# Score products on the diagonal 64x64 quarters of TensorE, V products on the other two, and 274 tiles kept off ScalarE

## The chip, the cores and the metric

The kernel runs on one core of a Trainium2 chip. The metric is the device time of one execution in microseconds (us); the time given is the median of three runs. One more execution was taken with the hardware profiler, and the trace is of that one.

## The reference, cut to what matters

The input is one image of 224 x 224 positions with C = 96 channels. Each position gives a query, a key and a value of 96 channels; the first 48 channels attend inside horizontal strips of 8 x 224 positions, the other 48 inside vertical ones.

```
sw, C2 = 8, C // 2
qkv = einsum('bhwc,cd->bhwd', x, wqkv);  q, k, v = three slices of C channels
# horizontal: 28 strips of 1792 positions, 48 channels
ah = softmax(einsum('bqc,bkc->bqk', qh, kh) * C2**-0.5)
oh = einsum('bqk,bkc->bqc', ah, vh)
# vertical: the same on 28 strips of 224 x 8 positions, the other 48 channels
ov = ...
out = einsum('bhwc,cd->bhwd', concat(oh, ov), wo)
```

In all, 56 strips of 1792 x 1792 scores, each of which needs an exponential: 180 million of them. The row sums come out of the V product, whose 49th column is a one.

## The kernel before, in words

**Tiling.** Two strips make a *pair* P; there are 28 pairs, 0 to 13 horizontal and 14 to 27 vertical. The keys and queries of the two strips of a pair lie on partitions 0 to 48 and 64 to 112 of `KT_sb` and `QT_sb` (index w = 0, 1). The queries of a pair are cut into four chunks c of 512, 512, 512 and 256. A *tile* is 128 keys x 512 queries x 2 strips (256 keys in the last chunk): 128 x 1024 scores in two PSUM banks. There are 49 tiles in a pair and 1372 in all.

**A tile on ScalarE.** TensorE makes the scores with four matmuls, one on each 64 x 64 quarter of its array (`qk_fn`, L761: strip w on 64 rows, key half kh on 64 columns). ScalarE takes exp of both banks at once into a bf16 tile `PT` (L939). TensorE then multiplies with V (`pv_fn`, L788): 128 keys on all 128 rows, one strip on 64 columns and the other on the other 64, so two matmuls a tile, which add up in one bank over the tiles of a chunk. ScalarE's tiles use two sets of two banks in turn (`SETS`), so that the scores of tile n+2 wait until ScalarE is through with tile n. The other four banks are a ring (`RING`): the bank in which the V product adds up, the score banks of the tiles off ScalarE, and the banks of the *fills*.

**A tile off ScalarE.** 251 tiles get their exponential elsewhere, as integer arithmetic on the bits of the scores. The table `KINDS` names them, a letter each. All of them make their scores twice (`s_fn`, L774). Kind P (155 tiles): VectorE pass 1 takes the low halves of the words into `qb` (L1082), GpSimd squares (L1110), adds a constant (L1111) and squares again (L1106); the scores are made again and VectorE pass 2 adds them in (L1087). Kind R (96 tiles) has a pass more on VectorE (L1084) and only one square on GpSimd.

**Fills** are the other products: keys, queries and values of the pair after the one at work (L589, L634), and the output projection (L703, from pair 14 on). VectorE copies each out of its bank.

**What sets the order.** `ORDER` has a string per pair; a letter is one step of TensorE: `q` scores of a ScalarE tile, `1` and `2` (or `3`, `4`) first and second scores of a tile off ScalarE, `v` one V product, `k`, `g`, `f` a fill. TensorE runs them exactly so. The orders of VectorE and GpSimd come from a planner in the program, which walks `ORDER` with durations and picks what is ready. Each engine waits on counters of the others, `emit` writes those waits, and every wait holds up all that is behind it on the engine.

Of the kernel before, what the change touches and what calls it, by code (L numbers as in the profile page):

```python
# [6 lines left out]
BF16 = mybir.dt.bfloat16  # L7
# [21 lines left out]
    ["PR", "P", "PPP", ""],  # L29
    ["RPR", "PP", "RRPRR", ""],  # L30
    ["PR", "P", "PPRR", ""],
    ["RRPP", "RP", "PRRP", ""],
    ["RP", "RP", "PPPRR", ""],
    ["PRR", "P", "PPPRR", ""],
    ["PPRR", "P", "PRPRP", ""],
    ["PRR", "P", "PPRP", ""],
    ["PR", "RRP", "PPPRRP", ""],
    ["RR", "PP", "PPRRP", ""],
    ["PRP", "PPPR", "RP", ""],
    ["RP", "P", "RPPPRR", ""],  # L40
    ["RPR", "P", "PPPRPR", ""],
    ["RRP", "P", "PPRRP", ""],
    ["PR", "RPPPR", "PR", ""],
    ["PP", "RRPPR", "P", ""],
    ["PPPR", "RPP", "RRPP", ""],
    ["PR", "PPPRP", "P", ""],
    ["PPR", "R", "PPRP", ""],
    ["PPPRR", "PP", "R", ""],
    ["PPPP", "RR", "PRPP", ""],
    ["PPR", "R", "PPPP", ""],  # L50
    ["PPP", "RRRPR", "PP", ""],
    ["PPR", "PP", "RRPP", ""],
    ["PR", "PPP", "RRPP", ""],
    ["PP", "PP", "PRR", ""],
    ["PPP", "RRPR", "RPP", ""],
    ["PP", "P", "PPRRPPP", ""],
]
NPT = 28
NQB = 5
NV2 = 1  # L60
# [7 lines left out]
SEMD, SEMP, SELF, SEMX = 0.15, 0.10, 0.19, 0.05  # L68
# [3 lines left out]
D_H, D_F, D_SQ, D_AF, D_M2 = 0.604, 1.137, 1.9, 1.03, 0.055  # L72
D_AW, D_AG = 2.1, 1.03
# [6 lines left out]
D_V2 = 0.6  # L80
# [15 lines left out]
    "vq2vqv1qvvkqvvvq1vqvkqkvq1qkvqvvq2qvvkqv2qkqkkqkqk1qvvkqvvqv1qvvqvvqv1qvvqkvvq2qvkvqv2qvvq1vvq2qvv2qvq2vvq1qvv2qvvqv2q",
    "vvq1vqvkq2vqkvq1qkvqvvkvq1qvvvqvvq2vqvkvqkqk1qvvq1qvkqkkq1qkvqvvq1vqvvqvv2qvqvvq2vqvv2qvvq2qvv1qvq2vvq1qvv2qvqkvvq1vvq2q",
    "vv2qvqv1qkvqvvvq1vqvkqkvq1qkvvqkvq2vqvkqkvvq1qvvgqkqkvgqgkqkvqv2qvvq2vqv1qvvq2vqv1qvvvqvq1vqvvqvv1qvqv2qkq2qvvq3vqvvq2vvq",
    "2qvv2qvvqkkqkq1vqkvvqvvkq1qvgvqkgqkqkvq2vqv1qvkqkvq1vqgvvqvgq2vqkvqkgvq2vqv2qvvq1vqgvq2vqv1qvvqvvq1vqvvqvv1qvvqgvqgvq1vqvvq2vq",
    "v2qvvq2vqv1qvgvqvvq1vqvvqvv2qvqkvqkvkqkvvq1qvvkq3qkvvq2vqv2qvvq4vqgvq2vqvkq1vqv1qvvqgvqvvqkgqkkqgqgvq1vvq4qkvvq2qkvvq",  # L100
    "2qv1qvvvqv1qvvq2vqvkqk2qvvqgvkq1qkvvqkvq1vqvkqkvqgvq4vqgvq1vqvkqk2qvvqkvq1vqkvqkvgq2vqv2qvvq2vqvgq1vqv1qvvgqvvqv1qvvqvvgqv4qvvq",
    "v1qvvqv2qvvq1vq4qvvkqkq1kqvvkqvvkq2qvvqkvvq3vqvgq4vqgvq2vqv2qvvqkvq1vqv1qgvqvkq2vqv2qkvqkvq1vqkvq1vqvvvqv1qvvqvvkqv4qvvqv4qvvq",
    "v1qvvq2vqv1qvvqk1qvvqkvvqvkqkvqggvqkgqk2qvvvq2vqv3qvvqg2qvvqv1qvgqvkq2vqv1qgvqvkq4vqvgq1vqkkqkvqv1qvvkqvgqvvq1vqvgvqvvq1vqvvq2vq",
    "vvvq2vqv2qvvqkkqk1qvqkvvqvvq2vqvvq1vkqv1qvkqv2qvvqk4qvvqvgq2vqv1qgvqkvq1vqkgqv4qvkqv1qkvqvvqvvq1vqvkvqvvq4vqvvq2vvqv1qvvq",
    "v2qvvq1vqv2qvkqkkqvvkqggqkvqg1qvkqkgqkqkkqkvvq2vqv1qvvq1vqgvq2vqv2qvvqv1qkvvq2vqv2qgvqv1qgvqv2qgvqv1qvvqvvgqv1qvvqvvqv1qvvvqvvq",
    "vvqv2qvvq1vqvkq2kqvvq1qvvkqvvqkvvq2qvv1qkvq3vqvvq2vqv2qgvqgvgqkvqkq2vqkvq1vqkkqv2qgvqv2qvkqv1qvvqkvgq1qgvvqvvq2vqvvq2vvq",
    "1qvvvqv1qvvq2vqv4qvvqk1qvkqvvvq1qvvvqvvq2vqvvqkkvqv1qvvqkgq1vqkvq2vqvkq2vqv1qgvqvkq2vqv4qvvqk1qvvqvkqvvkqgvq1qkvvq2vqv2qvvq",
    "1vqv2qvvqgvq1vqv4qvvqk1qkvqvvqv1qvvqvvq2vqvgqkvqgvkqgvvqk1qvvq1vqkvq2vqkvq2vqv1qgvqvkq2vqv1qvvqg2qvvqkkqgvgqgvqkkvqv2qvvq2vq",
    "v1qvvq1vqv2qvvvq2qvv1qvvqkkq1qvkvqvvkqv1qvqvvvq4qvvvqkgqgkqvvq2vqkvq1vqv1qgvqkvq2vqv2qvkqvkq4vqkvq1vqv1qvvgqvvqv1qvvqvvqgvqv2qvvq",
    "kvvq1vqv2qvvq2vqv1qvgvqvvq1vqvvqvvq1vqvkqkvkqvvq2vqkvqvkgq1vqkvq2vqv1qgvqkvq2vqv2qvgqvkqvgqg1qvvqkkqgvkq2qvkvqv1qvvq2vqv2q",  # L110
    "vvq1vqvvvq2vqv1qvvq1vqvvqv1qvvqvvvq2vqvgqgvqgvq1vqvvq2vqv2qvvq2vqv1qvvfqv1qvfqv2qvfqvvfqvvfqv2qvvfqgvqgvq2vqv2qvvgqfvq4fqqvvvvvfffvvvfff",
# [9 lines left out]
class Sched:  # L121
# [70 lines left out]
    def commit(self, eng, start, dur, lat, fn, reads, writes, fresh=(), tag=""):  # L192
        d = self.deps(eng, reads, writes)
# [24 lines left out]
def bass_standalone__window_attn_cswin__vision_kernel(  # L218
# [28 lines left out]
    with es:  # L247
# [21 lines left out]
        V_sb = [sb(f"V_sb{i}", [128, 2, NKT, CA], BF16) for i in range(2)]  # L269
        V2_sb = [sb(f"V2_sb{i}", [128, 2, NV2, CA], BF16) for i in range(2)]  # L270
# [136 lines left out]
        for i in range(2):  # L407
            pool_now(["vones"], lambda e, i=i: e.memset(V_sb[i][:, :, :, C2:CA], 1.0), 0.2)
# [147 lines left out]

        def wblk(P, kind):
            return {"k": 2, "v": 4}[kind] + ph_of(P)

        def wqT_fill(ph):  # L560
            def pe_fn(e, bk):
                for w in range(2):
                    ins = e.matmul(bk[64 * w:64 * w + 64, 0:C], lhsT=wq_sb[ph][0][0:C, 0, :], rhs=ident[0:C, 0:C],
                                   start=True, stop=True)
# [9 lines left out]
        HALVES = [(0, 64), (64, C + 1)]  # L574
# [3 lines left out]
        def prep_fills(P):  # L578
# [3 lines left out]
            for kind, L in (("k", K), ("q", Q)):  # L582
                for c in range(NCH):
                    q0, qs = CH_Q0[c], CH_SIZES[c]

                    def pe_fn(e, bk, kind=kind, q0=q0, qs=qs):
                        for w in range(2):
                            lw = w_sb[:, wblk(P, "k"), :] if kind == "k" else wq_sb[ph][b][:, w, :]
                            ins = e.matmul(bk[64 * w:64 * w + 64, 0:qs], lhsT=lw, rhs=xT_sb[b][0:C + 1, w, q0:q0 + qs],  # L589
                                           start=True, stop=True)  # L590
                        return ins
# [21 lines left out]
            def pe_fn(e, bk):  # L613
                for w in range(2):
                    for a, z in ((0, 64), (64, 128)):
                        ins = e.matmul(bk[a:z, w * k_n[P]:(w + 1) * k_n[P]], lhsT=wqT[ph][:, w, a:z], rhs=ksum[b][:, 0:k_n[P]], start=True, stop=True)
                return ins
# [7 lines left out]
            for k0 in range(0, 2 * NKT, VS):  # L625
                n = min(VS, 2 * NKT - k0)
                ws = sorted({k0 // NKT, (k0 + n - 1) // NKT})

                def pe_fn(e, bk, k0=k0, n=n):
                    for j in range(n):  # L630
                        w, kt = divmod(k0 + j, NKT)
                        for h in range(2):
                            t0 = kt * 128 + 64 * h
# [1000 lines left out]
```

## Time and profile before

| what | value |
|---|---|
| median of 3 runs | 1047.3 us (1047.17 to 1047.32) |
| the profiled execution, its own time | 1047.03 us |
| its span, first to last instruction | 1045.2 us |
| TensorE (PE) busy | 1024.8 us, 13456 matmuls |
| VectorE (DVE) busy | 1027.6 us |
| ScalarE (ACT) busy | 1034.9 us, of it 1030.3 us in 1121 exponentials |
| GpSimd (POOL) busy | 1001.9 us |
| granted TensorE clock | 0.999 |

A busy share says how much of the span has an instruction of the engine in it. The instructions of one engine overlap at their ends, so the step from one to the next is shorter than the duration of one; a busy share near 100% thus doesn't say by itself which engine sets the pace. The views used below are the page's parts, the timeline (instructions in order, merged where alike: start, length, engine, line, operation, tiles, count), the waits, one source line's instructions, and the stretches.

### The profile page before, as it was taken

To read this page: it belongs to the slowest core of one execution; us is meant where nothing else is said; L and a number is where in the kernel's file an instruction comes from. 1 tells how busy PE (TensorE), PEld (TensorE's weight loads), DVE (VectorE), ACT (ScalarE), POOL (GpSimd) and SP (SyncE) were. 2 spreads that over 40 slices of the span, in tenths; PEclk is the share of its full clock that TensorE was granted. 3 is DMA by queue.
4 is the path that set the end of the run, shared out by engine and by line. 5 is a ranking of instruction groups with operands and counts; after the bars stand their busy time and mean duration, and the time that the engine had idled before them with its cause. 6 is when DMAs were issued, how large, how long until landed. Compare 5 with 4: busy or idle time off the path is not lost.

```text
span 1045.2 us, 33013 instructions
## 1 busy us (share of the span) xinstructions
PE 1024.8 (98%) x13456; PEld 388.6 (37%) x13456; DVE 1027.6 (98%) x1905; ACT 1034.9 (99%) x1131; POOL 1001.9 (96%) x662
## 2 busy tenths in 40 slices
PE   9999999999999999999999999999999999999997
PEld 4333333333333333333333333334333333343333
DVE  8999999999999999999999999999999999999998
ACT  8999999999999999999999999999999999999997
POOL 7999999999999999999999999999999999999997
PEclk9999999999999999999999999999999999999999
DMA  8997718828863774132146355534525542552343
GB/s 175 166 181 126 131 24 140 119 52 125 147 93 71 130 108 81 28 59 59 15 91 114 60 93 103 101 58 94 95 49 104 105 100 44 104 102 49 71 79 60
DMA packets 414199, 96.84 MB, mean 93 GB/s; under 512 B 404928, under 2 KB 411296, under 8 KB 414048
## 3 DMA queue, kind: packets, MB, share of 16 engines
q1 hardware_dynamic: 413376, 94.11, 51.9%
q8 instruction: 105, 1.72, 0.7%
q10 hardware_dynamic: 544, 0.44, 0.1%
q14 instruction: 46, 0.38, 0.1%
q0 software_dynamic: 128, 0.20, 0.1%
HBM read 28.31 MB, written 28.21 MB: 54 GB/s over the span
## 4 chain that ended last, share of the span: by engine, by line
PE 59%; DVE 24%; ACT 8%; issue 4%; POOL 4%; DMA 1%; POOLq 0%; ACTq 0%; SPq 0%; DVEq 0%
PE ps L788 23%; PE ps L761 20%; PE ps L774 10%; ACT PT L939 8%; DVE qb L1082 7%; DVE PT L1087 7%; DVE PT L1084 3%; PE ps L589 3%; DVE KT_sb L594 2%; PE ps L703 2%; POOL PT L1106 2%; PE ps L634 2%; DVE OT_sb L958 1%; DVE QT_sb L603 1%; POOL PT L1110 1%
## 5 line engine op out<-in xcount | busy, mean ns | idle before, releaser
L939 ACT ACTIVATE PT<-ps 128x1024 bf16<-128x1024 f32 x1121 | 1030.3, 1091 | 0.6 <-PE ps L761 0.2
L1106 POOL TENSOR_TENSOR PT<-PT 128x1024 f16<-128x1024 f16 x251 | 470.4, 1893 | 8.6 <-DVE PT L1084 1.0
L788 PE MATMUL ps<-PT,V_sb 128*49 128x512 bf16 (+1 forms) x3136 | 470.1, 362 | 0.3 <-DVE PT L1087 0.2
L761 PE MATMUL ps<-QT_sb,KT_sb 49*64 49x512 bf16 (+1 forms) x5292 | 456.4, 361 | 2.6 <-ACT PT L939 1.5
L1082 DVE TENSOR_SCALAR qb<-ps 128x512 f16<-128x512 int16 x490 | 329.8, 697 | 3.2 <-PE ps L761 0.3
L1087 DVE SCALAR_TENSOR_TENSOR PT<-ps,PT 128x512 uint16<-128x512 f32 (+1 forms) x479 | 323.0, 709 | 5.2 <-PE ps L774 0.9
L1110 POOL TENSOR_TENSOR PT<-qb 128x1024 f16<-128x1024 f16 x155 | 291.9, 1892 | 9.8 <-DVE qb L1082 6.5
L761 PEld LDWEIGHTS ps<-QT_sb,KT_sb 49*64 49x64 bf16 x5292 | 136.9, 104 | 264.0 <-ACT PT L939 240.3
L774 PE MATMUL ps<-QT_sb,KT_sb 54*64 54x512 bf16 (+1 forms) x2008 | 202.6, 394 | 11.7 <-DVE PT L1087 2.7
L788 PEld LDWEIGHTS ps<-PT,V_sb 128*49 128x49 bf16 x3136 | 133.2, 103 | 202.6 <-issue 169.8
L1111 POOL TENSOR_SCALAR PT<-PT 128x1024 f16<-128x1024 f16 x155 | 161.8, 1044 | 13.0
L1084 DVE SCALAR_TENSOR_TENSOR PT<-ps,qb 128x512 f16<-128x512 int16 (+1 forms) x190 | 128.0, 688 | 0.6
L774 PEld LDWEIGHTS ps<-QT_sb,KT_sb 54*64 54x64 bf16 (+1 forms) x2008 | 56.8, 103 | 101.0 <-DVE PT L1087 34.2
L958 DVE CAST OT_sb<-ps 113x512 bf16<-113x512 f32 x111 | 68.5, 617 | 0.1
L603 DVE CAST QT_sb<-ps 128x512 bf16<-128x512 f32 (+1 forms) x111 | 67.5, 615 | 0.1
L594 DVE TENSOR_SCALAR_CACHE_REDUCE KT_sb<-ps 128x512 bf16<-128x512 f32 x108 | 64.4, 616 | 0.0
L709 DVE CAST og<-ps 128x480 bf16<-128x480 f32 x84 | 50.8, 616 | 0.2
L641 DVE CAST V_sb<-ps 128x480 bf16<-128x480 f32 (+1 forms) x84 | 50.8, 617 | 0.1
L589 PE MATMUL ps<-xT_sb,wq_sb 97*64 97x512 bf16 x224 | 41.5, 368 | 0.0
L589 PE MATMUL ps<-xT_sb,w_sb 97*64 97x512 bf16 x224 | 39.8, 369 | 0.0
L634 PEld LDWEIGHTS ps<-w_sb,xT_sb 96*64 96x64 bf16 x1568 | 33.6, 112 | 16.3 <-issue 7.5
L634 PE MATMUL ps<-w_sb,xT_sb 96*64 96x48 bf16 x1568 | 39.3, 190 | 0.0
(67 smaller groups left out, 236.4 us busy)
## 6 DMA issues: line engine op xcount, KB each, us to landing
xT_sb<-xt_dram SPq DMA_DIRECT2D x28, 336.0 KB, 5.2
out_dram<-og SPq DMA_DIRECT2D x190, 48.0 KB, 2.0
xp_dram<-in_x_dram SPq DMA_DIRECT2D x26, 336.0 KB
oc_all<-xp_dram SPq DMA_DIRECT2D x26, 336.0 KB, 4.6
xt_dram<-xT_sb SPq DMA_DIRECT2D x26, 336.0 KB, 6.4
oh_all<-ohn SPq DMA_DIRECT2D x52, 84.0 KB, 2.7
stg<-oh_all SPq DMA_DIRECT2D x13, 336.0 KB, 4.6
xt_dram<-xT_sb SPq DMA_DIRECT2D x4, 168.0 KB, 5.1
```

Of the source, the lines that this page charges most:

```text
L589: ins = e.matmul(bk[64 * w:64 * w + 64, 0:qs], lhsT=lw, rhs=xT_sb[b][0:C + 1, w, q0:q0 + qs], start=True, stop=True)
L634: ins = e.matmul(bk[64 * h:64 * h + 64, j * C2:(j + 1) * C2], lhsT=xT_sb[b][0:C, w, t0:t0 + 64], rhs=w_sb[0:C, wblk(P, "v"), 0:C2], start= ...
L761: ins = e.matmul(bank(SETS[s] + w)[64 * kh:64 * kh + 64, i * t["qs"]:(i + 1) * t["qs"]], lhsT=KT_sb[b][64 * w:64 * w + CA, kt * 128 + 64 * ...
L774: ins = e.matmul(bank(bp[w])[64 * kh:64 * kh + 64, 0:512], lhsT=KT_sb[b][64 * w:64 * w + nr, kt * 128 + 64 * kh:kt * 128 + 64 * kh + 64], ...
L788: ins = e.matmul(bank(pb)[64 * w:64 * w + CA, 0:t["qs"]], lhsT=V2_sb[b][:, w, kt - NKT + NV2, :] if second else V_sb[b][:, w, kt, :], rhs= ...
L939: S.commit("act", 0.0, D_ACT, None, lambda e, s=s, slot=slot: e.activation(PT[slot][:], ps[:, 512 * SETS[s]:512 * SETS[s] + 1024], ACTF.Ex ...
L1082: fn, reads, writes = lambda e: e.tensor_scalar(q, l, m, a, ALU.mult, ALU.add), bk, qk
L1084: fn, reads, writes = lambda e: e.scalar_tensor_tensor(y.bitcast(FP16), l, -RA * 2.0 ** 16, q, ALU.add, ALU.mult), bk + qk, ptk
L1087: fn, reads, writes = lambda e: e.scalar_tensor_tensor(y.bitcast(U16), f, 128.0, y.bitcast(FP16), ALU.mult, ALU.add), bk + ptk, ptk
L1106: square = ("pool", D_SQ, lambda e: e.tensor_tensor(y, y, y, ALU.mult), yk + ["pser"], yk)
L1110: return [("pool", D_SQ, lambda e: e.tensor_tensor(y, q, q, ALU.mult), qk, yk), ("pool", D_AF, lambda e: e.tensor_scalar(y, y, -(QS * (RB ...
L1111: ("pool", D_AF, lambda e: e.tensor_scalar(y, y, -(QS * (RB + RA) / 2) ** 2, 1.0, ALU.add, ALU.mult), yk + ["pser"], yk),
```

## The change

**Quarters.** A score tile now uses only the two diagonal quarters (rows 0 to 63 to PSUM partitions 0 to 63, rows 64 to 127 to 64 to 127). Its four matmuls go as two pairs, one after the other: pair a = 0 takes 64 keys of both strips into the first bank, pair a = 1 the next 64 keys into the second (`score_half`). So a strip, no longer a key half, owns 64 partitions of a `PT` tile. The V product uses the two other quarters: strip w on rows 64w, its output on the other half of the partitions, 64 keys at a time, so two pairs a tile here too (`pv_fn`). All products are now on 64 rows and 64 columns; before, scores were and all else was on up to 128 rows.

**Fills in two halves.** A fill has 96 or 97 rows, so it is split into 64 rows on one pair of quarters and the rest on the other pair. The letter `k`, `g` or `f` now issues the first half, on the diagonal; a new letter `j` issues the second (`end_fill`), which adds into the same bank and waits for the first half by TensorE's own counter.

**Tiles off ScalarE.** All 274 are of a kind Q that was in the program and not in use: pass 1 on VectorE, written to `PT` itself (no `qb`), one square on GpSimd, pass 2 on VectorE. The result is one of two approximate words, the other is the same word plus 64 in its integer form, made by GpSimd (`shifted`) into a second `PT` tile. Both get a V product, the second with values scaled by 0.707 (`V2_sb`, made by GpSimd once a pair). ScalarE keeps 1098 tiles. VectorE now always takes a tile in two halves of 512 columns. `PT` has 34 tiles instead of 28, `qb` none instead of 5.

```diff
-    ["PR", "P", "PPP", ""],
+    ["QQ", "Q", "QQQ", ""],
...
-NPT = 28
-NQB = 5
-NV2 = 1
+NPT = 34
+NQB = 0
+NV2 = 6
...
-    "vvq1vqv1qkvqvvq2qvvqkkvq1qkvqvkvq1vqvkqkqkvvq4qkvvq1qkqvvvq1vqvvvqv2qvvq1qvvq2qvvvq2vqv2qvvq2vqv1qvvq2vqkvkqvvq1vvq",
+    "v2vqvvqv1vqv1vqkjqvkjq1vqvkjq2vqvkjq1vq2vqvkjq1vq2vqvkvqj2vqvkvqvjqv1vqv2vqvvqv1vqv2vqvvqv1vqv2vqvkvqjkvqjkvjqv2vqkvjqv2vqvvkqv1vqvvqj1vq",
...
+        def split(part, n):
+            for w in range(2):
+                g = w if part == 0 else 1 - w
+                yield w, g, (0, 64) if g == 0 else (64, n)
...
-                        for w in range(2):
-                            lw = w_sb[:, wblk(P, "k"), :] if kind == "k" else wq_sb[ph][b][:, w, :]
-                            ins = e.matmul(bk[64 * w:64 * w + 64, 0:qs], lhsT=lw, rhs=xT_sb[b][0:C + 1, w, q0:q0 + qs],
-                                           start=True, stop=True)
+                        for w, g, (a, z) in split(part, C + 1) if part is not None else ((0, 0, (0, C + 1)), (1, 1, (0, C + 1))):
+                            lw = w_sb[a:z, wblk(P, "k"), :] if kind == "k" else wq_sb[ph][b][a:z, w, :]
+                            ins = e.matmul(bk[64 * w:64 * w + 64, 0:qs], lhsT=lw, rhs=xT_sb[b][a:z, 1 - w, q0:q0 + qs],
+                                           start=part != 1, stop=part != 0)
...
+        def score_half(e, t, a, bk, nr):
+            b, qs = t["P"] % 2, t["qs"]
+            for i, kb in half_of(t, a):
+                for w in range(2):
+                    p0 = 64 * w
+                    ins = e.matmul(bk[p0:p0 + 64, i * qs:(i + 1) * qs], lhsT=KT_sb[b][p0:p0 + nr, kb * 64:kb * 64 + 64],
+                                   rhs=QT_sb[b][p0:p0 + nr, t["q0"]:t["q0"] + qs], start=True, stop=True)
+            return ins
...
-                for i, kt in enumerate(t["kts"]):
-                    for w in range(2):
-                        ca = w * 512 + i * t["qs"]
-                        ins = e.matmul(bank(pb)[64 * w:64 * w + CA, 0:t["qs"]], lhsT=V2_sb[b][:, w, kt - NKT + NV2, :] if second else V_sb[b][:, w, kt, :],
-                                       rhs=PT[slot][:, ca:ca + t["qs"]],
+                for a in range(2):
+                    for i, kb in half_of(t, a):
+                        c0 = a * 512 + i * qs
+                        for w in range(2):
+                            r0, p0 = 64 * w, 64 * (1 - w)
+                            ins = e.matmul(bank(pb)[p0:p0 + CA, 0:qs],
+                                           lhsT=V2_sb[b][r0:r0 + 64, kb - 2 * NKT + 2 * NV2, :] if second else V_sb[b][r0:r0 + 64, kb, :],
+                                           rhs=PT[slot][r0:r0 + 64, c0:c0 + qs],
...
+                f["half"] = ("pe", S.cnt["pe"])
+            else:
+                S.commit("pe", 0.0, f["pe_dur"], f["pe_dur"] + L_FILL, lambda e, fn=f["pe_fn"], bk=bank(bi): fn(e, bk, 1),
+                         f["reads"], [("bank", bi)], after=[f["half"]])
...
-            return ("pool", D_AF, lambda e: e.tensor_scalar(w1, w0, 64.0, 1.0, ALU.add, ALU.mult), pt_keys(tl["slot"]) + ["pser"], pt_keys(tl["slot2"]))
+            return ("S", D_AF, lambda e: e.tensor_scalar(w1, w0, 1.0, 64.0, ALU.mult, ALU.add), pt_keys(tl["slot"]) + ["pser"], pt_keys(tl["slot2"]))
```

The durations in the planner's table are changed too, and with them the order on VectorE and GpSimd.

**TensorE, in pair 10, while the values of pair 11 are made.** Before: L761 is a ScalarE tile's scores, L774 those of a tile off ScalarE, L788 a V product, L634 a value fill.

```order
L634 MATMUL ps<-w_sb,xT_sb1 64x48 x20
L774 MATMUL ps<-QT_sb0,KT_sb0 64x512 [waits s_dve]
L774 MATMUL ps<-QT_sb0,KT_sb0 64x512 x3
L761 MATMUL ps<-QT_sb0,KT_sb0 64x512 [waits s_act]
L761 MATMUL ps<-QT_sb0,KT_sb0 64x512 x3
L788 MATMUL ps<-PT24,V_sb0 49x512 [waits s_dve]
L788 MATMUL ps<-PT24,V_sb0 49x512
L788 MATMUL ps<-PT27,V_sb0 49x512 x2
L761 MATMUL ps<-QT_sb0,KT_sb0 64x512 [waits s_act]
L761 MATMUL ps<-QT_sb0,KT_sb0 64x512 x3
```

Now, at the same work (L764 all scores, L786 a V product, L638 a value fill):

```order
L786 MATMUL ps<-PT26,V_sb0 49x512 x4
L638 MATMUL ps<-w_sb,xT_sb1 64x48 [waits s_dve]
L638 MATMUL ps<-w_sb,xT_sb1 64x48 x19
L786 MATMUL ps<-PT17,V_sb0 49x512 x4
L764 MATMUL ps<-QT_sb0,KT_sb0 64x512 [waits s_act]
L764 MATMUL ps<-QT_sb0,KT_sb0 64x512 x3
L638 MATMUL ps<-w_sb,xT_sb1 64x48 [waits s_pe]
L638 MATMUL ps<-w_sb,xT_sb1 64x48 x19
L764 MATMUL ps<-QT_sb0,KT_sb0 64x512 [waits s_dve]
L764 MATMUL ps<-QT_sb0,KT_sb0 64x512
L764 MATMUL ps<-QT_sb0,KT_sb0 64x512 [waits s_dve]
```

The V product has four matmuls instead of two; the fill appears twice with other steps between its halves, the second time behind a wait on TensorE's own counter (`s_pe`); a tile off ScalarE has a wait for each of its two banks.

**GpSimd, in pair 11, about the division of pair 10's rows.** Before: L1110 the first square and L1111 the constant of a P tile, L1106 the last square of a P or R tile, L1045 the division by the row sums.

```order
L1110 TENSOR_TENSOR PT25<-qb1 128x1024 [waits s_pe,s_dve]
L1111 TENSOR_SCALAR PT25<-PT25 128x1024 [waits s_pool]
L1106 TENSOR_TENSOR PT3<-PT3 128x1024 [waits s_dve]
L1106 TENSOR_TENSOR PT25<-PT25 128x1024 [waits s_pool]
L1045 TENSOR_TENSOR ohn<-OT_tr0,rn0 128x672 [waits s_dve,s_ot00,s_nc]
```

Now (L1079 the square, L1089 the second word, L1093 the scaled values, L1018 the division):

```order
L1079 TENSOR_TENSOR PT1<-PT1 128x1024 [waits s_dve]
L1089 TENSOR_SCALAR PT31<-PT26 128x1024 [waits s_act,s_pool,s_dve,s_pe]
L1089 TENSOR_SCALAR PT18<-PT21 128x1024 [waits s_pe,s_pool,s_act,s_dve]
L1093 TENSOR_SCALAR V2_sb0<-V_sb0 128x588 [waits s_dve]
L1018 TENSOR_TENSOR ohn<-OT_tr0,rn0 128x672 [waits s_nc,s_ot00]
L1089 TENSOR_SCALAR PT14<-PT1 128x1024 [waits s_pool,s_pe,s_dve]
```

A tile has one square and one second word, each on its own; the second word waits for the tile that it writes to be free of its last V product as well as for pass 2.

More of the change, by code (lines that the diff above doesn't have):

```diff
@@ L190, in fresh, with commit @@
         self.rd.pop(k, None)
-    def commit(self, eng, start, dur, lat, fn, reads, writes, fresh=(), tag=""):
-        d = self.deps(eng, reads, writes)
+    def commit(self, eng, start, dur, lat, fn, reads, writes, fresh=(), tag="", after=()):
+        d = self.deps(eng, reads, writes) | set(after)
         s0 = start
@@ L560, in wqT_fill, with pe_fn @@
         def wqT_fill(ph):
-            def pe_fn(e, bk):
-                for w in range(2):
-                    ins = e.matmul(bk[64 * w:64 * w + 64, 0:C], lhsT=wq_sb[ph][0][0:C, 0, :], rhs=ident[0:C, 0:C],
-                                   start=True, stop=True)
+            def pe_fn(e, bk, part):
+                for w, g, (a, z) in split(part, C):
+                    ins = e.matmul(bk[64 * w:64 * w + 64, 0:C], lhsT=wq_sb[ph][0][a:z, 0, :], rhs=ident[a:z, 0:C],
+                                   start=part == 0, stop=part == 1)
                 return ins
@@ L611, in prep_fills, with pe_fn @@
                                       [("QB", P)], ("Q", P, c)))
-            def pe_fn(e, bk):
+            def pe_fn(e, bk, part):
                 for w in range(2):
-                    for a, z in ((0, 64), (64, 128)):
-                        ins = e.matmul(bk[a:z, w * k_n[P]:(w + 1) * k_n[P]], lhsT=wqT[ph][:, w, a:z], rhs=ksum[b][:, 0:k_n[P]], start=True, stop=True)
+                    a, r0 = 64 * (w if part == 0 else 1 - w), 64 * w
+                    ins = e.matmul(bk[a:a + 64, w * k_n[P]:(w + 1) * k_n[P]], lhsT=wqT[ph][r0:r0 + 64, w, a:a + 64],
+                                   rhs=ksum[b][r0:r0 + 64, 0:k_n[P]], start=True, stop=True)
                 return ins
@@ L947, in emit_pv @@
             b = tl["P"] % 2
-            S.commit("pe", 0.0, D_MM, L_PV, pv_fn(tl, slot, first, last, pb),
+            S.commit("pe", 0.0, 2 * D_MM, D_MM + L_PV, pv_fn(tl, slot, first, last, pb),
                      pt_keys(slot) + (v_keys(b) if slot == tl["slot"] else [("V2", b)]),
@@ L1486, in do_fill @@
         def do_fill(c):
+            assert not open_fill
             f = dict(k=prep_q, f=fin_q, g=out_q)[c].pop(0)
```

384 lines of the change are left out of this document (158 added, 226 removed).

## The prediction

> **What bounds the kernel now.** I read the page's busy shares first, then the stretches for ScalarE, its timeline at both ends, the waits, and at last TensorE's timeline.
>
> ```profile
> span 1045.2 us, 33013 instructions
> PE 1024.8 (98%) x13456; PEld 388.6 (37%) x13456; DVE 1027.6 (98%) x1905; ACT 1034.9 (99%) x1131; POOL 1001.9 (96%) x662
> L939 ACT ACTIVATE PT<-ps 128x1024 bf16<-128x1024 f32 x1121 | 1030.3, 1091 | 0.6 <-PE ps L761 0.2
> ```
>
> Four engines are all but full, and ScalarE idles 0.6 us before its exponentials. The pace in the middle, from the stretches of L939:
>
> ```profile
> 20.00:520.00 500.00, 499.77 (x545) 1.00 0.60 98
> 520.00:1020.00 500.00, 499.95 (x545) 1.00 0.45 85
> ```
>
> 1000 us / 1090 = 0.917 us per tile. The two ends:
>
> ```profile
> 8.10 4.94 ACT L939 ACTIVATE PT<-ps 128x1024 bf16<-128x1024 f32 x5
> 1034.05 4.84 ACT L939 ACTIVATE PT<-ps 128x1024 bf16<-128x1024 f32 x5
> ```
>
> The first exponential starts at 8.10, the last ends at 1038.89. 1121 x 0.9174 = 1028.4; with 8.10 ahead and 6.3 behind it is 1042.8, and 2.4 us of the span are lost, mostly in the first tiles. So ScalarE sets the time: it never runs dry, and each tile taken off it is worth 0.917 us as long as the others follow. Who holds it up if they don't is in the waits:
>
> ```profile
> PEld ps L761 <- ACT PT L939: 240.3, 746, 0.8
> ```
>
> In 746 of 1121 score tiles it is TensorE that waits for ScalarE's banks.
>
> **ScalarE's share of the change.** 1098 tiles x 0.9174 = 1007.3 us, 21.1 us less. That is the gain on offer; the rest is whether TensorE, VectorE and GpSimd keep up with 1007 us.
>
> **The turn of a score tile.** A score tile is now two pairs in a row, where four matmuls went at once. The price of one more slot is seen in V products, two, six matmuls in a run, and in two slots of scores ahead of ScalarE:
>
> ```profile
> 100.22 0.83 PE L788 MATMUL ps<-PT,V_sb 128*49 128x512 bf16 x6
> 505.98 0.40 PE L788 MATMUL ps<-PT,V_sb 128*49 128x512 bf16 x2
> 12.53 0.63 PE L761 MATMUL ps<-QT_sb,KT_sb 49*64 49x512 bf16 x8
> 13.21 17.74 ACT L939 ACTIVATE PT<-ps 128x1024 bf16<-128x1024 f32 x19 [0.17 <-PE ps L761]
> 1035.92 1.14 ACT L939 ACTIVATE PT<-ps 128x1024 bf16<-128x1024 f32 x1
> 1037.12 0.41 PE L761 MATMUL ps<-QT_sb,KT_sb 49*64 49x256 bf16 x8 [0.51 <-ACT PT L939]
> L939 ACT ACTIVATE PT<-ps x1121: 1017/1081/1257, 8.1 to 1037.7; 128x1024 bf16<-128x1024 f32 x187
> ```
>
> (0.83 - 0.40) / 2 = 0.215 us a slot of 512 columns. The doubled tile at 12.53 has two slots and lets ScalarE start 0.68 later. From ScalarE's end (1035.92 + 1.14 = 1037.06) to the next score matmul are 0.06. Of the exponential the shortest takes 1.02. So the new turn of a set is 0.06 + 0.68 + 1.02 = 1.76 us for two tiles, where two tiles at ScalarE's pace are 1.83. The turn fits, with 0.07 to spare instead of 0.29: what reaches TensorE's scores later than that is now lost at ScalarE.
>
> **TensorE's load.** The work on one kind of quarter: scores of 1098 + 2 x 274 = 1646 tiles, and on the other V products of 1098 + 2 x 274 = 1646, each two slots: 1646 x 0.43 = 708 us on either. That both run beside each other is shown only in part. Four score matmuls at once (0.41 for x4 below, where x2 of V take 0.40) are four quarters streaming at once, and the two of a V product read different columns of the same rows at once; that pairs started at different times do so too no row shows. I take that they do, since each quarter in these rows needs nothing of the others.
>
> ```profile
> 503.47 0.39 PE L761 MATMUL ps<-QT_sb,KT_sb 49*64 49x512 bf16 x4
> 503.83 0.41 PE L589 MATMUL ps<-xT_sb,wq_sb 97*64 97x512 bf16 x2
> 504.38 0.41 PE L761 MATMUL ps<-QT_sb,KT_sb 49*64 49x512 bf16 x4
> 504.72 0.62 PE L788 MATMUL ps<-PT,V_sb 128*49 128x512 bf16 x4
> 505.27 0.41 PE L761 MATMUL ps<-QT_sb,KT_sb 49*64 49x512 bf16 x4
> ```
>
> What goes: the change between scores on 64 rows and V on 128. From 504.38 to 504.72 are 0.34 for one slot, from 504.72 to 505.27 are 0.55 for two: some 0.12 beyond the slots each way, and the old order changes 2010 times, about 240 us. That is what pays for the second slot of each tile. What is late next is the order itself: matmuls begin in program order, so a score pair whose quarter is taken holds back the V pair behind it.
>
> Fills add their halves to both sides: a key or query half is one slot, a value or output half about as much, 433 x 0.22 = 95 us. New is the wait of the second half: 0.41 (L589 above) until the first is through and 0.06 for the signal, so half two begins 0.47 or, with the signal's way to TensorE itself not in any row, up to 0.5 after half one. Behind it stand the scores for ScalarE. In the order 212 of 433 have a ScalarE score tile or more between the halves and cost nothing; 221 have none (86 of them a V product), and stall the scores by up to 0.5 - 0.215 = 0.29, 63 us in all at most, 0 at least.
>
> The stretches between two `q`: 548 hold one other score tile: 4 slots = 0.86 us. 427 hold a fill: 0.43 + 0.5 = 0.93 where the halves are close, less elsewhere. 125 hold neither. I walked the whole order with these numbers (a matmul begins once the one ahead has begun and its quarter is free, 0.215 a slot, 0.3 from the end of a half to its second): an estimate of 957 us, 0.87 a stretch, nine in ten at 0.95 or less. So TensorE has 50 us to spare in 1007, and evenly: what a stretch is late at 0.93 or 0.95 the next one at 0.86 makes good, and 0.03 lies within the 0.07 above.
>
> **VectorE.** Passes by halves: before 155 x 4 + 96 x 6 = 1196, now 274 x 4 = 1096.
>
> ```profile
> 480.04 2.50 DVE L1087 SCALAR_TENSOR_TENSOR PT<-ps,PT 128x512 uint16<-128x512 f32 x4
> L1082 DVE TENSOR_SCALAR qb<-ps 128x512 f16<-128x512 int16 x490 | 329.8, 697 | 3.2 <-PE ps L761 0.3
> ```
>
> Four in 2.50 with 0.69 for the last: 0.60 a half. 100 fewer are 60 us less, 968 of 1007. Pass 1 into `PT` rather than `qb` is the same form. Fills keep their copies.
>
> **GpSimd.**
>
> ```profile
> 488.00 3.75 POOL L1110 TENSOR_TENSOR PT<-qb 128x1024 f16<-128x1024 f16 x2
> 491.83 2.17 POOL L1111 TENSOR_SCALAR PT<-PT 128x1024 f16<-128x1024 f16 x2
> 494.08 7.45 POOL L1106 TENSOR_TENSOR PT<-PT 128x1024 f16<-128x1024 f16 x4
> ```
>
> A square is (7.45 - 1.89) / 3 = 1.85, a constant 2.17 - 1.04 = 1.13, with 0.13 more when it follows a square (491.83 + 2.17 = 494.00 to 494.08; 488.00 + 1.85 x 2 = 491.70 to 491.83). A P tile is 1.85 + 0.13 + 1.13 + 1.85 = 4.96, an R tile 1.85: 155 x 4.96 + 96 x 1.85 = 946. A Q tile is 1.85 + 0.13 + x, x the second word. No row has this form on 16-bit integers; the nearest, the constant, gives x = 1.13, the other end is a square, 1.85. With 1.13: 274 x 3.11 = 852; 28 scaled values at half a constant or so, 18. So 76 us less than now, 925 of 1007. With 1.85 it would be 1123. The second word also waits until its `PT` tile is through its last V product, and squares stand behind it; I take nothing for that, with 34 tiles where 28 and 5 `qb` did before, and a part of the 80 us to spare if it fails.
>
> **Ends, and SyncE.** The first six score tiles are doubled, four slots each now, so their turn is 0.06 + 0.68 + 0.43 + 1.02 = 2.19 for two tiles and costs about (2.19 - 1.83) x 3 = 1 us. The last fills are in halves too: about 1 us. SyncE issues the same transfers, a few in another order; none is waited for in the long waits. PE's spare time hides the new waits of the second banks; without that cover each is a part of a slot.
>
> **The sum.** 1007.3 + 8.1 + 6.3 + 2.4 lost as before + 2 at the ends = 1026.1 of span, 1.8 us around it as in the profiled execution (1047.0 against 1045.2), 1027.9. The median of before is 0.3 above the profiled execution. I forecast 1028.
>
> **Rivals.**
>
> *Weight loads lie bare, and TensorE becomes the bound: slower.* A pair that starts after a wait takes 0.41 instead of 0.39 (504.38 against 503.47): its weights were not loaded ahead. If with pairs alternating between quarters each pair pays that 0.02 to 0.024, the walk comes to 1034 us, above ScalarE's 1007, and with the 20.6 us around it the time is 1055. It decides from 0.015 a pair, where TensorE passes 1007. The Trainium skill speaks for it (TensorE: Matmul & The Clock Gate, section "The mechanism" in Part 3): weight loads overlap matmuls under way only where the row group differs, and scores and V products here share rows. This case's trace speaks against the rule:
>
> ```profile
> 504.72 0.13 PEld L788 LDWEIGHTS ps<-PT,V_sb 128*49 128x49 bf16 x4 [0.23 <-issue]
> ```
>
> All four loads of two V products, the second two for the same rows and columns as the first, are through in 0.13 us, while the first pair streams until 504.94. Chance 0.16, with other ways in which TensorE's order falls behind by 30 us.
>
> *ScalarE waits more often, gain half lost.* If the 0.07 to spare fails so that a tile takes 0.925 to 0.935, 1098 of them are 1016 to 1027, time 1036 to 1047. For it: scores now wait for VectorE's banks more tightly. Against: the stretches are even. Faster still, 0.19, or within the measurement's 0.2% (2 us), 0.04.
>
> *The second word is slow on GpSimd.* GpSimd without x: 274 x 1.98 + 18 + 55 (what it does besides, 1001.9 - 946) = 616. From x = 1.43 on it passes 1007; at 1.85 it is 1123 and the time about 1140. Chance 0.04.
>
> *The quarters don't overlap:* the change doesn't do what it says. Scores and V after each other are 1646 x 0.86 + 190 = 1606, time about 1625. Chance 0.03.
>
> **The numbers.** Forecast (1022 to 1036) 0.54; half lost 0.19; same 0.04; slower 0.16 + 0.04 + 0.03 = 0.23. Faster 0.73. A measurement of this kernel can tell about 0.2% from no change. Low: no loss at all, 1007.3 + 14.4 + 1.8 = 1023.5, less 1.5 for shorter ends. High takes in the bare weights, 1056. Outside are the last two rivals and a part of the first, under 0.2.
>
> **What would show it.** Right: L939 x1098 at 0.917 in the middle stretches and under 2 us idle before it; scores and V products of 0.4 us beside each other, starting 0.2 apart; GpSimd's second word at 1.04. Wrong: `PEld` waits for ScalarE near zero and ScalarE idle behind PE (bare weights or the order), L1089 far above 1.1 (second word), V pairs starting only as score pairs end (no overlap).

## The result, and the profile after

The changed kernel takes 1920.15 us, the median of four runs (1918.13 to 1922.94), against 1047.24 for the kernel before, 1.834 times as long (95% interval 1.8307 to 1.837). The forecast was 1028, with 1022 to 1056 as the range; it was wrong by 892 us.

The page of the changed kernel: span and busy shares, the granted clock in 40 slices, the chain of waits by engine and by line, and ScalarE's exponentials with the idle time before them.

```profile
span 1916.2 us, 47667 instructions
PE 1898.4 (99%) x20580; PEld 1113.9 (58%) x20580; DVE 996.0 (52%) x1841; ACT 1058.7 (55%) x1108; POOL 899.0 (47%) x677
PEclk8878788777888878878778677766867679576778
PE 98%; DVE 1%; issue 1%; ACT 0%; DVEq 0%
PE ps L764 27%; PE ps L638 26%; PE ps L786 26%; PE ps L705 14%; PE ps L594 5%; DVE PT L1060 0%; DVE PT L1055 0%; ACT PT L944 0%; PE ps L432 0%; PE ps L812 0%; DVE OT_sb L965 0%; PE ps L672 0%; DVE og L684 0%; PE ps L621 0%; DVE og L711 0%
L944 ACT ACTIVATE PT<-ps 128x1024 bf16<-128x1024 f32 x1098 | 1053.9, 1033 | 848.0 <-PE ps L764 485.2
```

ScalarE, VectorE and GpSimd are busy half the time, and ScalarE sits idle for 848 us where it was 0.6. The chain that ended last is 98% TensorE. In it the value fills (L638) and the output fills (L705) hold 26% and 14%, together 40% x 1916 = 766 us. These are small products: 48 and 96 columns each. The clock that TensorE was granted (`PEclk`, in tenths of full speed) lies between 0.5 and 0.9 in the slices; its mean over the execution is 0.768, where it was 0.999.

Now TensorE's timeline of the changed kernel. The first row is a value fill, the second an output fill, the third what ScalarE does about the time of the second (start, length, engine, line, operation, tiles, count; in brackets the wait ahead of it):

```profile
905.95 2.53 PE L638 MATMUL ps<-w_sb,xT_sb 64*64 64x48 bf16 x17
901.43 1.64 PE L705 MATMUL ps<-wo,oc_all 32*64 32x96 bf16 x10
903.50 3.77 ACT L944 ACTIVATE PT<-ps 128x1024 bf16<-128x1024 f32 x4 [2.84 <-PE ps L786]
```

A single one of these matmuls takes 0.23 or 0.245 from start to end (the groups below). So from one start to the next are (2.53 - 0.23) / 16 = 0.144 us in the value fill and (1.64 - 0.245) / 9 = 0.155 in the output fill, although a matmul of 48 columns has a tenth of the columns of a slot of 512. ScalarE had waited 2.84 us.

A lowered clock isn't what makes these steps long. The stretches of the two fills and of a third, with the granted clock behind the busy times (for PE, PEld, DVE, ACT, POOL), and the third in the timeline:

```profile
905.95:908.89 2.94, 2.94 (x30) 2.01 (x27) 0.99 (x2) 1.32 (x2) 2.07 (x2) 1.00 0.03 6
901.43:903.07 1.64, 1.64 (x16) 1.09 (x18) 0.00 (x0) 0.00 (x0) 1.10 (x1) 1.00 0.00 0
842.98:846.00 3.02, 3.02 (x22) 2.01 (x17) 0.68 (x2) 1.02 (x1) 1.89 (x1) 0.50 0.00 0
843.00 3.19 PE L638 MATMUL ps<-w_sb,xT_sb 64*64 64x48 bf16 x18
```

The first two ran at the full clock, 1.00. The third ran at 0.50, and its step is (3.19 - 0.24) / 17 = 0.17 us, with 0.24 for a single one. All through this trace the granted clock is either 1.00 or 0.50; the digits of the slices are means of the two.

The same lines in the groups of the changed kernel by form, rows x columns of the weights ahead of the tile that streams:

```profile
L638 PE MATMUL ps<-w_sb,xT_sb 64*64 64x48 bf16 x1568 | 360.9, 233 | 0.0
L638 PE MATMUL ps<-w_sb,xT_sb 32*64 32x48 bf16 x1568 | 362.1, 231 | 0.2
L705 PE MATMUL ps<-wo,oc_all 32*64 32x96 bf16 x784 | 191.4, 244 | 1.1
```

Half of a fill's matmuls have 64 rows and half have 32: `split(part, C)` cuts 96 rows into 64 and 32, and the loop issues them by turns, 64, 32, 64, 32. Apart from four matmuls with the identity (L570), nothing else in the kernel has 32 rows: a key or query fill has 97, so its second piece has 33.

### The profile page after: what moved, and what is told of

Same layout as the page of the kernel before. It is cut to its first block, busy times and chain, and to the rows that moved or that the text cites. A ratio compares the mean times of both kernels' runs of the same rounds, so it can differ in the third digit from the quotient of the medians.

```text
span 1916.2 us, 47667 instructions
## 1 busy us (share of the span) xinstructions
PE 1898.4 (99%) x20580; PEld 1113.9 (58%) x20580; DVE 996.0 (52%) x1841; ACT 1058.7 (55%) x1108; POOL 899.0 (47%) x677
## 4 chain that ended last, share of the span: by engine, by line
PE 98%; DVE 1%; issue 1%; ACT 0%; DVEq 0%
PE ps L764 27%; PE ps L638 26%; PE ps L786 26%; PE ps L705 14%; PE ps L594 5%; DVE PT L1060 0%; DVE PT L1055 0%; ACT PT L944 0%; PE ps L432 0%; PE ps L812 0%; DVE OT_sb L965 0%; PE ps L672 0%; DVE og L684 0%; PE ps L621 0%; DVE og L711 0%
## 5 line engine op out<-in xcount | busy, mean ns | idle before, releaser
L764 PE MATMUL ps<-QT_sb,KT_sb 49*64 49x512 bf16 (+3 forms) x7392 | 1028.3, 416 | 1.3 <-ACT PT L944 0.2
L786 PE MATMUL ps<-PT,V_sb 64*49 64x512 bf16 (+1 forms) x7368 | 1013.8, 411 | 0.1
L1079 POOL TENSOR_TENSOR PT<-PT 128x1024 f16<-128x1024 f16 x274 | 516.2, 1892 | 353.8 <-DVE PT L1055 314.0
L764 PEld LDWEIGHTS ps<-QT_sb,KT_sb 49*64 49x64 bf16 (+2 forms) x7392 | 381.6, 119 | 247.0 <-issue 56.2
L638 PE MATMUL ps<-w_sb,xT_sb 32*64 32x48 bf16 (+1 forms) x3136 | 516.4, 232 | 0.2
L638 PEld LDWEIGHTS ps<-w_sb,xT_sb 32*64 32x64 bf16 (+1 forms) x3136 | 364.2, 117 | 219.7 <-issue 80.0
L786 PEld LDWEIGHTS ps<-PT,V_sb 64*49 64x49 bf16 x7368 | 393.3, 111 | 77.4 <-issue 16.5
L1089 POOL TENSOR_SCALAR PT<-PT 128x1024 uint16<-128x1024 uint16 x274 | 285.7, 1044 | 270.4 <-DVE PT L1060 149.1
L1055 DVE TENSOR_SCALAR PT<-ps 128x512 f16<-128x512 int16 x548 | 350.9, 683 | 64.5 <-PE ps L764 43.7
L1060 DVE SCALAR_TENSOR_TENSOR PT<-ps,PT 128x512 uint16<-128x512 f32 x548 | 351.7, 681 | 32.6 <-PE ps L764 16.1
L705 PE MATMUL ps<-wo,oc_all 32*64 32x96 bf16 (+1 forms) x1568 | 286.4, 245 | 1.4 <-DVE PT L1055 0.2
L705 PEld LDWEIGHTS ps<-wo,oc_all 32*64 32x64 bf16 (+1 forms) x1568 | 171.9, 110 | 150.6 <-issue 47.8
L1093 POOL TENSOR_SCALAR V_sb<-V_sb 128x588 bf16<-128x588 bf16 x28 | 19.1, 681 | 342.0 <-DVE V_sb L643 342.0
L965 DVE CAST OT_sb<-ps 113x512 bf16<-113x512 f32 x111 | 68.7, 619 | 36.1 <-PE ps L764 23.0
```

The source lines that it names most:

```text
L638: ins = e.matmul(bk[64 * w:64 * w + 64, j * C2:(j + 1) * C2], lhsT=xT_sb[b][a:z, 1 - w, t0:t0 + 64], rhs=w_sb[a:z, wblk(P, "v"), 0:C2], st ...
L705: ins = e.matmul(bk[64 * h:64 * h + 64, s * C:(s + 1) * C], lhsT=oc_T[b][a:z, 4 * (m // 2) + 2 * h + m % 2, :].rearrange("c (t u) -> c u t ...
L764: ins = e.matmul(bk[p0:p0 + 64, i * qs:(i + 1) * qs], lhsT=KT_sb[b][p0:p0 + nr, kb * 64:kb * 64 + 64], rhs=QT_sb[b][p0:p0 + nr, t["q0"]:t[ ...
L786: ins = e.matmul(bank(pb)[p0:p0 + CA, 0:qs], lhsT=V2_sb[b][r0:r0 + 64, kb - 2 * NKT + 2 * NV2, :] if second else V_sb[b][r0:r0 + 64, kb, : ...
L965: S.commit("dve", 0.0, 0.6, 0.75, lambda e: e.tensor_copy(OT_sb[P % 2][0:64 + CA, q0:q0 + qs], bank(pb)[0:64 + CA, 0:qs]), [("bank", pb)], ...
L1055: fn, reads, writes = lambda e: e.tensor_scalar(q, l, m, a, ALU.mult, ALU.add), bk, qk
```

## The experiments

**The question.** The theory: each change between a matmul of 64 rows and one of 32 costs TensorE some 0.14 us, since it finishes what is under way first, and 33 rows count with the 64. Against it stands what else the new fills brought: many small matmuls on all four quarters, between scores and V products that hold these quarters, and a lowered clock that makes all of it slow. By that a row more or another order inside a fill would change little. Counted in the trace, 2014 matmuls have another size than the one ahead of them in the kernel before (nearly all 128 rows against 64), and 4672 in the changed one (nearly all 32 against 64).

**e1_rows33: 33 rows instead of 32, in both fills.** The extra row of the weights holds zeros. Shown are the loop of the value fill, that of the output fill, and the zero row for the latter; the fills also wait for those rows to be written.

```diff
-                        for w, g, (a, z) in split(part, C):
+                        for w, g, (a, z) in split(part, C + 1):
...
-                        for h, g, (a, z) in split(part, C):
+                        for h, g, (a, z) in split(part, C + 1):
...
+            pool_now(["wo6z"], lambda e: e.memset(wo6[C:C + 1, :], 0.0), 0.12)
```

> The changed kernel, but the second piece of a value fill or output fill has 33 rows (row 96 multiplied by a zero row) where it had 32; same number of matmuls, same order, same waits. Theory A (a 32-row piece makes TensorE change the size of its tiles, and each change costs 0.13 to 0.17 us): the 0.14 to 0.17 us steps between matmuls of a fill go to about 0.03, TensorE's clock comes back to 0.99, and the time is what the prediction's other terms give, 1022 to 1040 us. Theory B (small matmuls on two different row groups into one bank are slow in themselves, whatever their rows): steps stay over 0.1 us, 1800 us or more. Theory C (the granted clock, for power with four quarters at work, is the cause): clock stays under 0.85, 1300 us or more.

Measured: 1034.61 us (1033.82 to 1035.3), 0.9875 of the kernel before (0.9858 to 0.9891). The page, and a value fill in TensorE's timeline:

```profile
span 1032.3 us, 47668 instructions
PE 1012.7 (98%) x20580; PEld 594.5 (58%) x20580; DVE 974.5 (94%) x1841; ACT 1018.8 (99%) x1108; POOL 897.0 (87%) x678
PEclk9999999999999999999999999999999999999999
L945 ACT ACTIVATE PT<-ps 128x1024 bf16<-128x1024 f32 x1098 | 1014.1, 1045 | 3.9 <-PE ps L765 2.0
L639 PE MATMUL ps<-w_sb,xT_sb 64*64 64x48 bf16 (+1 forms) x3136 | 72.4, 187 | 0.4
L706 PE MATMUL ps<-wo,oc_all 33*64 33x96 bf16 (+1 forms) x1568 | 61.0, 204 | 2.1 <-PE ps L787 0.2
569.49 0.49 PE L639 MATMUL ps<-w_sb,xT_sb 64*64 64x48 bf16 x20
```

The same 20580 matmuls in the same order, with one row more in 2352 of them, and 1920.15 - 1034.61 = 885.5 us are gone. A value fill's 20 matmuls take 0.49 us: (0.49 - 0.19) / 19 = 0.016 from one to the next, a ninth of 0.144. The clock is full, ScalarE idles 3.9 us. There are 12 changes of size left. Neither the number of small matmuls nor the quarters that they share is the cause, and the lowered clock goes with the 32 rows too.

**e2_grouped: 32 rows kept, but sorted.** In each half all pieces of 64 rows go first, then all of 32, in both fills; this is the value fill's edit.

```diff
-                    for j in range(n):
-                        for w, g, (a, z) in split(part, C):
+                    for w, g, (a, z) in sorted(split(part, C), key=lambda y: y[1]):
+                        for j in range(n):
```

> The changed kernel with its 32-row pieces, but within a half of a fill all 64-row pieces go first and then all 32-row pieces, instead of turn by turn. Theory A (each change of tile size costs): two changes in a half instead of 10 to 20, 336 halves x 2 x 0.14 = 94 us of changes, and TensorE's drained quarters beside them: 1060 to 1200 us. Theory A2 (a 32-row matmul is slow in itself, 0.14 us each): 2352 x 0.14 = 330 us stay, 1300 us or more. Theory C (clock): as the changed kernel, over 1700 us.

Measured: 1191.03 us in one run. The value fill's groups by form:

```profile
L638 PE MATMUL ps<-w_sb,xT_sb 64*64 64x48 bf16 x1568 | 75.8, 186 | 0.2
L638 PE MATMUL ps<-w_sb,xT_sb 32*64 32x48 bf16 x1568 | 78.8, 186 | 0.0
```

The very same matmuls as in the changed kernel, of 32 rows too, are now busy for 79 us instead of 362: not the 32 rows are dear, the turn is. 684 changes are left, 672 more than in e1_rows33, for 156.4 us: 0.23 each. Not all of that is the price of a change. Counted in the traces from one start to the next, a change from inside a fill takes 0.13 us here, and matmuls of one size in a fill are 0.037 apart where e1_rows33 has 0.017: some 80 of the 156 us stand in these steps and not in the changes. A likely reason is the sorting itself, by which one quarter at a time has all the work of a fill. In the value fills they are 0.032 apart with 64 rows and 0.034 with 32, so this, too, isn't a price of the 32 rows.

**e3_value33: 33 rows in the value fills alone.** The output fills, which run from pair 14 on, keep 64 and 32.

> The changed kernel with 33 rows in the value fills alone; the output fills (pairs 14 to 27) keep 32-row pieces. Theory A: the first half of the program runs at ScalarE's pace, 0.917 us a tile; in the second some 1400 changes of 0.14 to 0.17 us are left, about 220 us beyond what TensorE has to spare: 1200 to 1290 us. Theory C: over 1600 us.

Measured: 1340.27 us in one run, 50 us above what was expected. The page's slices, and the stretches of ScalarE's exponentials (start:end, length, busy time and count, granted clock, DMA share and GB/s):

```profile
ACT  8999999999999999667756666475657574756565
PEclk9999999999999999789988788697889897778788
20.00:520.00 500.00, 498.97 (x543) 1.00 0.58 100
700.00:1320.00 620.00, 392.27 (x409) 0.84 0.25 51
```

Where only value fills run, the pace is 543 tiles in 500 us, where e1_rows33 has 542 in the same stretch; from the slice in which the output fills begin, ScalarE falls to 0.66 tiles a us and TensorE's clock to 0.84. 1542 changes are left, 1530 more than in e1_rows33, for 305.7 us: 0.20 each. For the changed kernel it is 4660 more for 885.5 us: 0.19 each. Three kernels with 672, 1530 and 4660 changes thus give 0.23, 0.20 and 0.19 us for one, of which 0.144 and 0.155 stand in the timeline rows directly. The theory holds. The expected 1200 to 1290 us for e3_value33 went by 0.14 to 0.17 a change; missed was that the clock falls too, and that an output fill's change takes 0.158 at the full clock and 0.216 at half of it (counted in the trace).

**What the repaired change still lacks.** e1_rows33 is 6.6 us over the forecast's 1028. TensorE's longest waits (us in total, times, longest):

```profile
PEld ps L765 <- ACT PT L945: 57.5, 249, 0.5
PEld ps L765 <- DVE PT L1056: 55.9, 168, 0.5
PEld ps L595 <- PE ps L595: 50.2, 125, 0.5
PEld ps L765 <- DVE PT L1061: 40.4, 135, 0.5
```

TensorE waits for ScalarE's banks 249 times, where it was 746, so it is later than ScalarE far more often. Two waits could make it late: for its own first half (L595 for L595: a fill's second half), or for VectorE's banks (L1056 and L1061, the two passes). Theory A of the next experiment says the first; the other reading is the second.

**e4_late_half: e1_rows33 with fewer close halves.** Where `j` stands right ahead of `q`, ScalarE's scores now go first, when they can: 11 fills instead of 221 have no score of ScalarE between their halves.

```diff
+        for n in range(len(todo) - 1):
+            if todo[n] == "j" and todo[n + 1] == "q":
+                todo[n] = "J"
...
+            if c == "J":
+                if can_q():
+                    late.append(1)
+                    continue
...
+            if c == "q" and late:
+                late.pop()
+                do_q()
...
+                c = "j"
```

So a half that can be put off is issued right behind the next `q`. The planner walks the new order, so VectorE's and GpSimd's orders can shift with it.

> The kernel with 33-row pieces (e1_rows33, 1034.6 us); where the second half of a fill stands just ahead of a ScalarE tile's scores, the scores now go first. Of 433 second halves 11 instead of 221 have no ScalarE scores since their first half. Theory A (the wait of a second half for its first one stalls the scores behind it, as the prediction has it, and that is a good part of the 10 us that ScalarE waits in e1): TensorE's wait for its own first half (50 us at L595 in e1) falls to under 15 us, 1026 to 1031 us. Theory B (ScalarE's waits in e1 come from VectorE's banks and from single late steps): no change, 1033 to 1037 us, or slower since fills are copied later.

Measured: 1042.77 us (1041.04 to 1043.75), 0.9952 of before (0.9937 to 0.9967), so 8 us slower than e1_rows33.

```profile
PEld ps L765 <- ACT PT L945: 82.6, 295, 0.6
PEld ps L765 <- DVE PT L1056: 69.5, 182, 1.0
PEld ps L765 <- DVE PT L1061: 60.9, 164, 0.5
```

The wait of L595 for its own first half is no longer among the listed waits, and the time is longer all the same: the waits for VectorE's banks grew from 55.9 + 40.4 to 69.5 + 60.9 us. A likely reason is that a fill whose halves lie apart holds its bank of the ring longer; no run tests that by itself. Theory A falls; the other reading fits, but VectorE's passes themselves were not made shorter, so that the rest would go with them is argued, not shown.

**e5_near_half: e1_rows33 with every second half right behind its first.**

```diff
-        for c in "".join(ORDER):
+        for c in "".join(ORDER).replace("j", "").replace("k", "kj").replace("g", "gj").replace("f", "fj"):
```

> The kernel with 33-row pieces; every second half of a fill comes directly behind its first half, 433 without cover instead of 135. Theory A: 212 more stalls of up to 0.29 us and 86 that lose their V product, 60 to 80 us more for TensorE, which had 50 to spare: 1045 to 1075 us. Theory B (the waits are hidden in TensorE's spare time): 1034 to 1040 us.

Measured: 1103.36 us in one run, 68.7 more than e1_rows33 and above the 1075 that was expected at most. The first row is from the groups, the others from the waits:

```profile
L945 ACT ACTIVATE PT<-ps 128x1024 bf16<-128x1024 f32 x1098 | 1038.6, 1032 | 48.4 <-PE ps L787 24.1 <-PE ps L765 9.0 <-PE ps L706 1.9
PEld ps L595 <- PE ps L595: 81.4, 172, 0.6
PEld ps L765 <- ACT PT L945: 45.9, 169, 0.7
```

Where a key or query fill's second half waits for its first, it waits 81.4 / 172 = 0.47 us, close to the prediction's 0.47 from half to half, and without work between the halves ScalarE pays for it: 48.4 us idle. In the order, 212 more fills have no score of ScalarE between their halves and 86 others lose a V product there: 68.7 us over these 298 are 0.23 each, over the 212 alone 0.32, a little above the prediction's bound of 0.29. The expectation had 60 to 80 us more for TensorE and let the 50 us that TensorE had to spare take most of it up. They didn't: TensorE still waits 45.9 us for ScalarE at other places, while ScalarE idles here. What is spare in one stretch doesn't make good what is late in another. So the cover of halves matters, and of the three orders tried the changed one is the best: closer costs 69 us, wider 8.

**e6_no_twice and e7_33_once: single scores for the first tiles.** `NTWICE` set to 0, so that the first six score tiles are not made twice: e6_no_twice from e4_late_half, e7_33_once from e1_rows33.

```diff
-NTW0, NTWICE = 1, 6
+NTW0, NTWICE = 1, 0
```

> e4_late_half, and the first six score tiles are no longer made twice. Theory A (the doubled tiles now cost four slots in a turn and hold ScalarE up, as the prediction has it, about 1 us): 1 us less than e4. Theory B (without them TensorE's clock falls in the first microseconds): the same or more than e4.

> The kernel with 33-row pieces (e1_rows33, 1034.6 us), and the first six score tiles no longer made twice. Theory A (four slots in a turn hold ScalarE up at the start): about 1 us less lost in the first 20 us, 1033 to 1034 us, and no clock loss. Theory B (TensorE's clock needs them): the clock is low in the first slices, 1035 us or more.

Measured: 1044.49 us (1043.23 to 1046.72; 0.9966 of before, 0.9952 to 0.998) and 1034.9 us (1033.53 to 1035.58; 0.9881, 0.9865 to 0.9898). Neither differs from the kernel that it was made from by more than their runs differ, which is 1.5 to 3.5 us: a gain of 1 us, as the prediction had it for the doubled tiles, can't be told by these runs. The fastest version found is the change with 33 rows, with or without them.

## Why the prediction was wrong

**The term that failed.** The prediction's load of TensorE has the term "a value or output half about as much, 433 x 0.22 = 95 us", and nothing for changes of size in the new order. Measured are 766 us of the chain in L638 and L705 where that term allowed under 95. The step behind it is in the description of the change: "All products are now on 64 rows and 64 columns". That holds for the scores, the V products, the keys and the queries; it doesn't for 96 rows split at 64, of which 32 are left. The diff shows it in one line, `(0, 64) if g == 0 else (64, n)` with n = 96 for values and outputs, against n = 97 for keys and queries.

**The price was known, the count was not made.** The same part of the prediction reads from the kernel before that a change of size costs "some 0.12 beyond the slots each way", counts 2010 of them there, and books their going as what pays for the second slot of each tile. It took the new kernel's count as nothing. Counted, it is 4672. Had the 1568 pairs of value matmuls and 784 pairs of output matmuls been counted, with two changes a pair, 4704 x 0.12 = 564 us on top of the walk's 957 would have put TensorE at 1521, far above ScalarE's 1007. The Trainium skill (TensorEngine Tiling (Array Packing), section "Key Properties") says: "Changing tiling mode (not just tile) drains the TensorE", and its section "When to Use Tiling" puts a contraction of 32 rows in another mode than one of 64; these runs agree, at 0.14 to 0.16 us for one change. That 33 rows go with 64, e1_rows33 shows.

**Where the rest went.** The 885.5 us can be split by counting, in the traces of the changed kernel and of e1_rows33, the time from each matmul's start to the next one's. The steps that begin at a value or output matmul take 756 us in the changed kernel and 98 in e1_rows33, 658 more. All other steps take 1156 us and 930, 226 more. So about three quarters of the loss stands in the fills themselves, and a quarter in scores, V products and the other fills, which are the same in both kernels. Of the 1156 us, 414 ran at a granted clock of 0.50; between matmuls outside the small fills a step takes 0.095 us there and 0.059 at 1.00, an estimated 3698 x 0.036 = 133 us of the 226. The change into a fill is most of the rest: 0.29 us at the full clock and 0.54 at half, where a step into a fill takes 0.07 in e1_rows33. The lower clock comes with the changes of size: in e3_value33 it is 1.00 in the stretch without them and 0.84 in the stretch with them, and it is back in e1_rows33. With 684 of them, in e2_grouped, the page has 9 in every slice. TensorE is listed as 98 or 99% busy in the kernel before, the changed one and e1_rows33 alike; the busy share doesn't see that it stands still between two sizes.

**The rivals.** None named this. Bare weight loads at the price of the first rival would have given 1055 us; e1_rows33 has every pair of the changed kernel, takes 1034.6, and ScalarE idles 3.9 us in it. A smaller price isn't ruled out: in e1_rows33 the chain that ended last is 95% TensorE, where it was 59% in the kernel before, and the 3.9 us are over the 2 that the prediction gave as a sign of being right. The second word is as forecast, in the row of e1_rows33:

```profile
L1090 POOL TENSOR_SCALAR PT<-PT 128x1024 uint16<-128x1024 uint16 x274 | 285.5, 1044 | 48.3 <-DVE PT L1061 20.1
```

That is 1.04 us a word, as long as the constant took before, from whose row the prediction had its step of 1.13: the lower end of its bound. The quarters do overlap, as TensorE's timeline of the changed kernel shows between two fills:

```profile
902.84 0.40 PE L764 MATMUL ps<-QT_sb,KT_sb 49*64 49x512 bf16 x2
902.86 0.42 PE L786 MATMUL ps<-PT,V_sb 64*49 64x512 bf16 x2
903.08 0.38 PE L764 MATMUL ps<-QT_sb,KT_sb 49*64 49x512 bf16 x2
903.09 0.41 PE L786 MATMUL ps<-PT,V_sb 64*49 64x512 bf16 x2
903.30 0.38 PE L764 MATMUL ps<-QT_sb,KT_sb 53*64 53x512 bf16 x2
903.31 0.41 PE L786 MATMUL ps<-PT,V_sb 64*49 64x512 bf16 x2
```

A pair of scores and a pair of V products start together, and the next two 0.22 later: four quarters stream at once. That step, which the rows of the kernel before showed only in part, was right.

**The rest of the sum, by e1_rows33.** There the rest can be read, since the failed term is gone. ScalarE's two ends in its timeline:

```profile
8.57 1.97 ACT L945 ACTIVATE PT<-ps 128x1024 bf16<-128x1024 f32 x2 [0.28 <-PE ps L765]
1014.11 12.17 ACT L945 ACTIVATE PT<-ps 128x1024 bf16<-128x1024 f32 x13
```

From 8.57 to 1026.28 are 1017.7 us for 1098 tiles, where the prediction had 1007.3 and 2.4 lost in them: 8 us more. The pace in the middle, in the same stretches as in the prediction:

```profile
20.00:520.00 500.00, 498.87 (x542) 1.00 0.58 100
520.00:1020.00 500.00, 498.02 (x540) 1.00 0.46 86
```

That is 1000 / 1082 = 0.924 us a tile instead of 0.917. It is the prediction's second rival, "the 0.07 to spare fails", a little below its 0.925 to 0.935: TensorE's turn is tight. The waits for VectorE's banks and for own halves may be what pushes some tiles past it; that is argued, not shown. The start of 8.57 instead of 8.10 and the 6.0 behind the end instead of 6.3 nearly cancel. With 1.9 around the span the profiled execution took 1034.2, inside the 1022 to 1036 that had the chance of 0.54, but near its slow end and with a part of the second rival in it. One kernel can't say whether the chance was well set.

## What to carry to other kernels

Before products are put on parts of TensorE's array, list the rows of every matmul in the new order, the small fills included, and count how often the size changes from one to the next: each change costs some 0.14 us here, with matmuls of 48 columns, and in the two kernels with 1542 and 4672 of them the granted clock fell as well. A remainder of 32 rows beside pieces of 64 can be padded with one row of zeros, which took 885.5 us off here, or sorted so that the sizes meet rarely, which took off 729. A price found in the kernel before ("a change costs 0.12") has to be multiplied with the count in the kernel after, not only with the count that goes away.

## What the runs showed of the hardware

Four quarters sustain one pair of 512 columns each 0.215 us or little more on both kinds at once (rows at 902.84 to 903.30), and a matmul of 48 columns follows another of its size in 0.016 us (e1_rows33). A change between 64 and 32 rows takes nine times that, by the timeline rows 0.144 and 0.155 us at the full granted clock and 0.17 at half of it. A stream full of such changes was granted a TensorE clock of 0.768 on a single core, as a mean of stretches at 1.00 and at 0.50, with TensorE listed as 99% busy. The change thus has its price without the lower clock, and the lower clock goes when 32 rows become 33; by what way the changes bring it about, the records don't show.
